# Attention and two expert layers on one core: scale and shift of the negated row maximum on ScalarE

## Chip, core, metric

The program runs on one core of a Trainium2 chip. The time is device microseconds of one execution; lower is better. TensorE (PE) multiplies, VectorE (DVE), ScalarE (ACT) and GpSimd (POOL) work element by element, SyncE (SP) issues the transfers (DMA).

## What is computed

Attention over 4 batches, 8 heads, 576 positions and 64 columns per head, with a mask by blocks of 64 positions, then a mixture of 4 expert layers on the 2304 x 512 result, then a second layer with a softmax, a normalisation and a last product. Of the attention, cut to what matters:

```python
scores = scale * np.matmul(q, k.transpose(0, 1, 3, 2))       # scale = 1/8
scores = np.where(mask, scores, -1000000000.0)
scores = scores - np.max(scores, axis=-1, keepdims=True)
attn = np.exp(scores)
attn = attn / (np.sum(attn, axis=-1, keepdims=True) + 1e-09)
return np.matmul(attn, v)
```

## The kernel before

The 2304 rows are 18 tiles of 128. Attention walks through 84 steps, `Attention.steps`. A step is a tile and some of its heads: four heads for the two tiles of first blocks (4 steps), two heads for tiles with index 1 to 3 (48 steps), one head for tiles with index 4 (32 steps).

A step goes through three functions. `step_a` has PE write the scores into a PSUM tile `sps` (`ps`; its pool `pss` has two buffers) and then, in its inner function `rest`, has DVE take the negated row maximum into the small tile `nm` (lines 923, 925, 927) and, on line 928, multiply it by 1/8 and add 14 ln 2, in place. `step_b` has ACT write exp(scores/8 + nm) into `p32` (line 959; the pool `pp` has two buffers), with the row sum as a second, small instruction; then ACT copies it as the high half into the f16 tile `hl` (line 963), DVE writes the low half by a subtraction (line 964, which frees the `p32` buffer), and SP issues a transposing transfer of `hl` into `pT`. `step_c` has PE multiply `pT` by the values (line 993, tile `pv`), one or two steps later, and `finish` normalises a tile and hands it to the expert layers.

A loop after the class weaves these steps with the units of the first expert phases (lines 372, 382, 383 for the hidden layer, lines 394, 414, 419 for its output), and with loading and splitting the weights (lines 129, 140, 232, 235 and, on POOL, 228). This woven part lasts until about 505 us. After it come the other expert phases and the second layer, which hold no attention.

Each engine runs its own queue in order. The order of a queue is not the order of the source: the context is opened with `schedule_with_timeline_sim=True`, so a planner lays out the queues by priority and by its own simulated times, and sets the semaphores. The evacuations of the expert layers have a raised priority (`tc.high_priority(offset=PRI)`). PE's `psh` pool for the hidden layer has three PSUM buffers.

Of the kernel before, what the change touches and what calls it, by code (L numbers as in the profile page):

```python
# [7 lines left out]
F32 = mybir.dt.float32  # L8
# [6 lines left out]
AF = mybir.ActivationFunctionType  # L15
ALU = mybir.AluOpType
# [7 lines left out]
SCALE = 1.0 / HD ** 0.5  # L24
BIG = 2.0 ** 50
PRI = 2000
PBITS = 14
LSC = 2.0 ** 10
OLAG = 4
LN2 = 0.6931471805599453  # L30
# [30 lines left out]
def tile_kernel(  # L61
# [38 lines left out]
    vec, act, gp, sync = nc.vector, nc.scalar, nc.gpsimd, InOrder(nc.sync)  # L100
    NPH = 3

    cp = ctx.enter_context(tc.tile_pool(name="const", bufs=1))
# [16 lines left out]
    pt = cp.tile([128, NTILE, E], F32, name="pt")  # L120
    iw = cp.tile([128, 18], F32, name="iw")
    gl = cp.tile([128, KF], F32, name="gl")
    x2i = cp.tile([128, NTILE], F32, name="x2i")

    def squares(x, out, junk=None):
# [615 lines left out]
    class Attention:  # L741
# [136 lines left out]
        def step_a(self, n):  # L878
            t, p, heads, _ = self.steps[n]
            b, i = TILES[t]  # L880
            ps = self.pss.tile([128, 2, 512], F32, tag="s", name="sps")
            self.sPS[n] = ps
            nm = sp.tile([128, 4], F32, tag="nm", name="nm")
            self.nm_[n] = nm
            nh = len(heads)
            L = 64 + 128 * i
            mms = []
            if i == 0:
                v4 = ps[:, 0].rearrange("p (h c) -> p h c", h=4)
                hi, lo = self.qS[t, p]  # L890
                ks = self.kS["z", b, p]
                for h in range(4):
                    o = v4[:, h]
                    pe.matmul(o, hi[:, h], ks[:, h], start=True, stop=False)
                    pe.matmul(o, lo[:, h], ks[:, h], start=False, stop=False)
                    pe.matmul(o, mr, mc, start=False, stop=True)
            else:
                for j, h in enumerate(heads):
                    even = h % 2 == 0
                    hi, lo = self.qS[t, h // 4]  # L900
                    k0 = S - L if even else 0
                    if i < 4:
                        cuts = [(ps[:, j, 0:L], k0, L)]
                    else:
                        cuts = [(ps[:, a, 0:288], k0 + 288 * a, 288) for a in range(2)]
                    for x, (o, c, w) in enumerate(cuts):
                        rhs = self.kS[b, h][:, c:c + w]
                        masked = (x == 0) if even else (x == len(cuts) - 1)
                        om = o[:, 0:64] if even else o[:, w - 64:w]

                        def high(o=o, q=hi[:, h % 4], rhs=rhs):
                            pe.matmul(o, q, rhs, start=True, stop=False)  # L912

                        def low(o=o, q=lo[:, h % 4], rhs=rhs, masked=masked, om=om):
                            pe.matmul(o, q, rhs, start=False, stop=not masked)  # L915
                            if masked:
                                pe.matmul(om, mr, mc[:, 64:128], start=False, stop=True)

                        mms += [high, low]

            def rest():
                if i == 0:
                    vec.tensor_reduce(out=nm, in_=v4, axis=AX.X, op=ALU.max, negate=True)
                elif i < 4:
                    vec.tensor_reduce(out=nm[:, 0:2], in_=ps[:, :, 0:L], axis=AX.X, op=ALU.max, negate=True)
                else:
                    vec.tensor_reduce(out=nm[:, 0:1], in_=ps[:, :, 0:288], axis=AX.XY, op=ALU.max, negate=True)
                vec.tensor_scalar(  # L928
                    out=nm[:, 0:nh], in0=nm[:, 0:nh], scalar1=SCALE, scalar2=PBITS * LN2, op0=ALU.mult, op1=ALU.add
                )  # L930

            return mms, rest

# [256 lines left out]


    vec.memset(ones, 1.0)

    vec.memset(mr, 0.0)
    vec.memset(mc, 0.0)
# [385 lines left out]
```

## Time and profile before

| | us |
|---|---|
| median of 3 runs (1112.07 to 1114.56) | 1113.18 |
| the profiled execution | 1114.37 |
| its span, first to last instruction | 1112.6 |
| PE busy | 1048.0 (94%) |
| DVE busy | 797.7 (72%) |
| ACT busy | 514.1 (46%) |
| POOL busy | 182.1 (16%) |

The profiled execution took 1.77 us more than its span and lies 1.19 us above the median. Timeline rows give the start, the duration, the engine, line and operation, the tiles (written <- read), shapes and count, and in brackets how long the engine stood idle before it and what ended that. `PEclk` is the granted TensorE clock as a share of full speed. The chain is the work that ended last, followed back from the last instruction.

### The profile page before, as it was taken

To read this page: it belongs to the slowest core of one execution; us is meant where nothing else is said; L and a number is where in the kernel's file an instruction comes from. 1 tells how busy PE (TensorE), PEld (TensorE's weight loads), DVE (VectorE), ACT (ScalarE), POOL (GpSimd) and SP (SyncE) were. 2 spreads that over 40 slices of the span, in tenths; PEclk is the share of its full clock that TensorE was granted. 3 is DMA by queue.
4 is the path that set the end of the run, shared out by engine and by line. 5 is a ranking of instruction groups with operands and counts; after the bars stand their busy time and mean duration, and the time that the engine had idled before them with its cause. 6 is when DMAs were issued, how large, how long until landed. Compare 5 with 4: busy or idle time off the path is not lost.

```text
span 1112.6 us, 20532 instructions
## 1 busy us (share of the span) xinstructions
PE 1048.0 (94%) x8064; PEld 657.2 (59%) x8064; DVE 797.7 (72%) x1758; ACT 514.1 (46%) x1107; POOL 182.1 (16%) x176
## 2 busy tenths in 40 slices
PE   4579889799999999999999999999999999999998
PEld 4456666465555556555576767666667674444443
DVE  7898788738768677436677656674879558999883
ACT  5667676646755455433443424232446453333222
POOL 4874633422115421000000000000000000000000
PEclk9999989799999999999999999999999999999999
DMA  9868987928877857332531212330344311434333
GB/s 303 247 164 159 249 184 163 222 79 192 193 120 178 177 147 157 64 61 48 174 114 58 77 39 76 115 133 29 95 138 128 107 27 29 95 86 88 74 85 85
DMA packets 225600, 137.95 MB, mean 124 GB/s; under 512 B 184544, under 2 KB 192736, under 8 KB 225504
## 3 DMA queue, kind: packets, MB, share of 16 engines
q1 hardware_dynamic: 225504, 136.65, 50.2%
q8 instruction: 63, 1.03, 0.4%
q14 instruction: 33, 0.27, 0.1%
HBM read 79.47 MB, written 12.06 MB: 82 GB/s over the span
## 4 chain that ended last, share of the span: by engine, by line
PE 75%; DMA 9%; DVE 7%; POOL 4%; issue 2%; ACT 2%; SPq 0%; ACTq 0%; DVEq 0%; POOLq 0%
PE ops L394 29%; PE hps L626 13%; PE hps L372 11%; PE h L1432 8%; PE o L1495 8%; DMA pT<-hl 6%; PE pv L993 3%; PE sps L912 2%; DVE hl L964 1%; PE sps L915 1%; DVE wt L235 1%; POOL wt L228 1%; DMA spill<-acc 1%; POOL ks L792 1%; POOL qlo L792 1%
## 5 line engine op out<-in xcount | busy, mean ns | idle before, releaser
L394 PE MATMUL ops<-wt,hch 128*128 128x512 f16 x1728 | 396.1, 381 | 3.7 <-DVE wt L235 1.6
L394 PEld LDWEIGHTS <-hch 128*128 128x128 f16 x1728 | 166.8, 98 | 189.9 <-issue 11.0
L372 PE MATMUL hps<-xT,wt 128*128 128x384 f16 (+1 forms) x1536 | 216.3, 291 | 2.1 <-DVE hch L383 1.3
L372 PEld LDWEIGHTS <-wt 128*128 128x128 f16 x1536 | 126.9, 100 | 62.1 <-issue 6.7
L959 ACT ACTIVATE p<-sps,nm 128x320 f32<-128x320 f32 (+4 forms) x144 | 79.0, 553 | 78.3 <-DVE nm L928 58.7
L964 DVE TENSOR_TENSOR hl<-p,hl 128x320 f16<-128x320 f32 (+4 forms) x132 | 92.3, 718 | 30.4 <-ACT hl L963 29.8
L626 PEld LDWEIGHTS <-S 128*128 128x128 f16 x1152 | 96.0, 98 | 2.8 <-issue 0.5
L1432 PE MATMUL h<-wt,x2T 128*128 128x512 f16 x432 | 95.5, 379 | 1.8 <-DVE acc L419 1.8
L1495 PE MATMUL o<-wt,lt 128*128 128x512 f16 x432 | 95.5, 379 | 0.0
L235 DVE SCALAR_TENSOR_TENSOR wt<-stage,ws,wt 128x1024 f16<-128x1024 f32 (+1 forms) x64 | 85.3, 1346 | 6.1 <-ACT wt L232 4.4
L419 DVE SCALAR_TENSOR_TENSOR acc<-ops,coef,acc 128x512 f32<-128x512 f32 x54 | 40.4, 747 | 67.2 <-PE ops L394 67.1
L912 PE MATMUL sps<-ks,qhi 128*128 128x288 f32 (+3 forms) x160 | 70.6, 443 | 18.1 <-ACT p L959 7.8
L639 ACT ACTIVATE stu<-hps 128x384 f32<-128x384 f32 x72 | 34.5, 484 | 94.7 <-PE hps L626 94.6
L626 PEld LDWEIGHTS <-wt 128*128 128x128 f16 x864 | 72.9, 98 | 6.5 <-issue 0.6
L626 PE MATMUL hps<-T,S 128*128 128x192 f16 x864 | 76.5, 246 | 0.0
L383 DVE SCALAR_TENSOR_TENSOR hch<-hps,hch 128x384 f16<-128x384 f32 (+1 forms) x98 | 53.0, 541 | 29.8 <-ACT hch L382 29.6
L1432 PEld LDWEIGHTS <-x2T 128*128 128x128 f16 x432 | 42.3, 98 | 52.9 <-issue 2.1
L993 PE MATMUL pv<-v,pT 128*128 128x64 f16 x1392 | 54.8, 196 | 19.1 <-DMA pT<-hl 19.0
L1495 PEld LDWEIGHTS <-lt 128*128 128x128 f16 x432 | 42.3, 98 | 51.0
L382 ACT ACTIVATE hch<-hps 128x384 f16<-128x384 f32 (+1 forms) x98 | 47.1, 480 | 47.7 <-PE hps L372 47.4
L232 ACT ACTIVATE wt<-stage,ws 128x1024 f16<-128x1024 f32 (+1 forms) x56 | 59.8, 1094 | 18.8 <-DVE ws L140 15.2
L993 PEld LDWEIGHTS <-pT 128*128 128x128 f16 x1392 | 50.1, 100 | 30.1 <-DMA pT<-hl 23.0
(158 smaller groups left out, 1480.6 us busy)
## 6 DMA issues: line engine op xcount, KB each, us to landing
stage<-in_w_dram SPq DMA_DIRECT2D x50, 512.0 KB, 6.0
raw<-in_qT_dram SPq DMA_DIRECT2D x34, 256.0 KB, 3.4
vraw<-in_vC_dram SPq DMA_DIRECT2D x30, 256.0 KB, 3.3
raw<-in_kT_dram SPq DMA_DIRECT2D x24, 288.0 KB, 3.6
raw<-in_w_dram SPq DMA_DIRECT2D x24, 256.0 KB, 4.0
raw<-in_w_in_dram SPq DMA_DIRECT2D x8, 512.0 KB, 4.7
raw<-in_w_out_dram SPq DMA_DIRECT2D x8, 512.0 KB, 4.3
stage<-wf SPq DMA_DIRECT2D x8, 512.0 KB, 6.1
```

The lines of the kernel that those rows point to most:

```text
L232: h = paced_a(bg_(act.activation(out=hi, in_=r, func=AF.Copy, scale=stage[key, "s"]), "A"))
L235: stage["last"] = vec.scalar_tensor_tensor(out=lo, in0=r, scalar=stage[key, "s"], in1=hi, op0=ALU.mult, op1=ALU.subtract)
L372: pe.matmul(ps[:, j * n:j * n + n], w[:, a, kk, f * 128:(f + 1) * 128], x[:, b * KD + kk, c0:c0 + n], start=(m == 0), stop=(m == 3 * KD - 1),)
L383: marks["D"] = nc.vector.scalar_tensor_tensor(out=h[:, 1, :n], in0=ps[:, :n], scalar=0.0, in1=h[:, 0, :n], op0=ALU.max, op1=ALU.subtract)
L394: pe.matmul(ps, hch[f][:, a, o0:o0 + 128], w[:, b, f, :], start=(m == 0), stop=(m == 3 * KF - 1))
L626: i = pe.matmul(ps[x][:, jj * HT:jj * HT + HT], lhs(a, kk, jj), rhs(b, kk), start=start, stop=(m == 5), skip_group_check=not first or jj > 0,)
L912: pe.matmul(o, q, rhs, start=True, stop=False)
L959: act.activation(out=dst, in_=src, func=AF.Exp, bias=nm[:, j + x:j + x + 1], scale=SCALE, accum_out=sums[:, h:h + 1],)
L964: anc["D"] = vec.tensor_tensor(out=hl[:, W + c0:W + c0 + n_], in0=pf[:, 0:n_], in1=hl[:, c0:c0 + n_], op=ALU.subtract)
L993: pe.matmul(o, tt[:, a * nch + c, :], v[:, bb, hs], start=(m == 0), stop=(m == total - 1))
L1432: pe.matmul(ps[:, half], x[:, a * KD + kk, c:c + 128], w[:, b, kk, half * 512:half * 512 + 512], start=(m == 0), stop=(m == 3 * KD - 1),)
L1495: pe.matmul(ps, tt[:, a * KF + f], w[:, b, f], start=(m == 0), stop=(m == 3 * KF - 1))
```

## The change

Line 928's VectorE instruction is taken out. In its place ScalarE runs an `Identity` activation on the same tile in place, with the same scale and with the shift read from a constant one-column tile `cb`, which VectorE fills once at the start. The maxima stay on VectorE, and the exponentials read `nm` as before.

```diff
+    cb = cp.tile([128, 1], F32, name="cb")
...
-                vec.tensor_scalar(
-                    out=nm[:, 0:nh], in0=nm[:, 0:nh], scalar1=SCALE, scalar2=PBITS * LN2, op0=ALU.mult, op1=ALU.add
-                )
+                act.activation(out=nm[:, 0:nh], in_=nm[:, 0:nh], func=AF.Identity, bias=cb, scale=SCALE)
...
     vec.memset(ones, 1.0)
+    vec.memset(cb, PBITS * LN2)
```

## Rows read from the trace of the kernel before

**Rows 1.** The page: PE's total, and the granted clock in 40 slices.

```profile
PE 1048.0 (94%) x8064; PEld 657.2 (59%) x8064; DVE 797.7 (72%) x1758; ACT 514.1 (46%) x1107; POOL 182.1 (16%) x176
PEclk9999989799999999999999999999999999999999
```

**Rows 2.** Busy time by stretch: engine and instructions, clock, DMA share, GB/s.

```profile
0.00:50.00 50.00, 21.59 (x132) 19.64 (x132) 39.05 (x92) 29.74 (x89) 31.86 (x39) 1.00 0.90 274
50.00:207.00 157.00, 132.73 (x1565) 99.72 (x1564) 128.48 (x253) 107.44 (x270) 85.84 (x76) 0.95 0.84 191
207.00:505.00 298.00, 292.53 (x2271) 169.67 (x2271) 191.34 (x396) 156.05 (x363) 64.44 (x63) 0.99 0.65 139
505.00:1112.60 607.60, 601.18 (x4102) 368.15 (x4100) 438.80 (x1019) 220.85 (x388) 0.00 (x0) 1.00 0.32 87
```

**Rows 3.** Line 928: durations (min/median/max, ns), and who waited for it (us, times).

```profile
L928 DVE TENSOR_SCALAR nm<-nm x84: 133/156/1220, 10.4 to 504.4; 128x2 f32<-128x2 f32 x48, 128x1 f32<-128x1 f32 x32, 128x4 f32<-128x4 f32 x4
  ACT p L959: 58.7, 31
```

**Rows 4.** ACT's groups by shape: busy us, mean ns, idle before.

```profile
L959 ACT ACTIVATE p<-sps,nm 128x576 f32<-128x576 f32 x32 | 23.6, 738 | 32.8 <-DVE nm L928 30.4 <-DVE x2i L137 1.0 <-DVE hl L964 0.9
...
L959 ACT ACTIVATE p<-sps,nm 128x128 f32<-128x128 f32 x16 | 5.7, 365 | 4.8 <-DVE nm L928 3.4 <-DVE vinv L133 0.8 <-PE sps L917 0.5
...
L788 ACT ACT_TABLE_LOAD x1 | 1.3, 1283 | 0.7 <-PEq L1570 0.7
```

**Rows 5.** Timeline of DVE at 367 us, then ACT: a step without a queue.

```profile
367.41 0.75 DVE L927 TENSOR_REDUCE nm<-sps 128x1 f32<-128x576 f32 x1
368.19 0.15 DVE L928 TENSOR_SCALAR nm<-nm 128x1 f32<-128x1 f32 x1
...
368.44 0.74 ACT L959 ACTIVATE p<-sps,nm 128x576 f32<-128x576 f32 x1 [1.83 <-DVE nm L928]
```

**Rows 6.** Timeline of DVE at 69 us, then ACT: a scale queued behind others.

```profile
69.47 0.81 DVE L925 TENSOR_REDUCE nm<-sps 128x2 f32<-128x640 f32 x1
...
74.58 0.97 DVE L928 TENSOR_SCALAR nm<-nm 128x2 f32<-128x2 f32 x1
...
75.64 0.53 ACT L959 ACTIVATE p<-sps,nm 128x320 f32<-128x320 f32 x1 [1.43 <-DVE xi L133]
```

**Rows 7.** Timeline of DVE at 85 us, then ACT: a scale behind a subtraction.

```profile
84.90 1.07 DVE L925 TENSOR_REDUCE nm<-sps 128x2 f32<-128x896 f32 x1
88.21 0.62 DVE L964 TENSOR_TENSOR hl<-p,hl 128x448 f16<-128x448 f32 x1 [2.23 <-ACT hl L963]
88.75 0.16 DVE L928 TENSOR_SCALAR nm<-nm 128x2 f32<-128x2 f32 x1
...
89.03 0.64 ACT L959 ACTIVATE p<-sps,nm 128x448 f32<-128x448 f32 x1 [0.39 <-DVE nm L928]
```

**Rows 8.** Timeline of DVE at 178 us, then ACT: ACT itself is queued.

```profile
178.56 0.16 DVE L928 TENSOR_SCALAR nm<-nm 128x2 f32<-128x2 f32 x1
...
179.73 0.71 ACT L1046 ACTIVATE xh<-xf,xs 128x512 f16<-128x512 f32 x1
180.34 0.62 ACT L959 ACTIVATE p<-sps,nm 128x448 f32<-128x448 f32 x1
```

**Rows 9.** The chain (start, us, what): first two and last piece of line 928.

```profile
14.56 0.58 DVE nm L928
...
74.66 0.57 DVE nm L928
...
185.51 0.08 DVE nm L928
```

**Rows 10.** Timeline of DVE at the start: the first work after the constants.

```profile
5.41 0.69 DVE L792 TENSOR_TENSOR kz<-kv,kz 64x512 fp32r<-64x512 f32 x1 [3.68 <-POOL kz L790]
```

**Rows 11.** PE's longest pause after 50 us, and the stretch around it as windows.

```profile
203.15 1.46 PE L993 MATMUL pv<-v,pT 128*128 128x64 f16 x24 [4.32 <-DMA pT<-hl]
...
197.90:211.60 13.70, 9.38 (x53) 6.33 (x53) 11.79 (x29) 11.63 (x24) 10.53 (x10) 0.50 1.02 217
```

## The prediction, made before the changed kernel was built or run

> **What bounds the kernel now.** I read the page first. PE is busy for 94% of the span, so a change off PE can only win where PE stands idle or slow [rows 1]. The digits of the granted clock tell that full speed was granted nearly throughout, with two dips, in slices 6 and 8, that is between 139 and 223 us [rows 1]. Next I cut the span into four stretches [rows 2]. From 505 us on there is no attention, and PE is busy for 601.18 of 607.6 us. From 207 to 505 us attention runs beside the expert layers, and PE is busy for 292.53 of 298 us. PE's idle time lies ahead of that: 28.4 of the first 50 us, and 24.3 of the 157 us from 50 to 207. In that second stretch DVE is busy for 128.48 of 157 us, ACT for 107.44, and the transfers take 0.84 of the DMA engines [rows 2]. So the edit can count between 0 and 207 us; behind that, PE's own work sets the pace.
>
> Then I asked for line 928 itself. It runs 84 times, its median is 156 ns and its longest 1220 ns, and in 31 places ACT's exponential stood idle for it, 58.7 us in all [rows 3]. That sum looks like the prize, and it is not: it counts the whole time for which ACT was idle, with the waiting for PE's scores and for the maximum in it, and most of it lies where ACT is not the bound.
>
> **The change part by part.**
>
> *Removed:* 84 small DVE instructions. In a step with free queues the maximum ends at 368.16 (367.41 + 0.75), the scale runs from 368.19 to 368.34, and the exponential starts at 368.44: 0.28 us from the end of the maximum [rows 5].
>
> *Added:* 84 ACT instructions of one to four columns. The trace has no such shape. The exponential, which also takes a scale and a column of biases, takes 738 ns for 576 columns and 365 for 128 [rows 4]; the straight line through these has 0.83 ns per column and meets zero columns at 258 ns. I take 0.26 us, an estimate from these two rows; it is bounded by 0.37 us above (the shortest exponential, [rows 4]) and 0.13 us below (the shortest scale on DVE, [rows 3]). With the 0.10 us of the hand-over that the rows show (368.34 to 368.44, [rows 5]) and 0.04 us more until the exponential can read the result, a free step would need 0.40 us in place of 0.28: each such step gets 0.12 us slower, not faster.
>
> The Trainium skill speaks against this change: "ScalarE: Activation LUTs", section Rules for kernel authors, wants multiplications and additions on VectorE. Its fixed price for an ACTIVATE with a column of biases, about 0.28 us, would make a free step 0.42 us, beside the 0.40 from rows; the trace agrees that a free step loses, and the sum below changes by 0.04 us.
>
> *What moves:* the gain can only come from steps where the scale was queued on DVE. In 53 of the 84 steps other DVE instructions stand between the maximum and its scale. At 69.47 the maximum starts and is done at 70.28, but the scale runs at 74.58 and takes 0.97 us; the exponential follows at 75.64 [rows 6]. Without the queue on DVE it could start about 1.3 us earlier, behind ACT's own work, which ends at about 74.2. At 84.90 it looks alike: the maximum is done at 85.97, the scale runs at 88.75. But ahead of it stands a subtraction of line 964 that had waited for ACT, and that subtraction ends at 88.83 and frees the `p32` buffer that the exponential at 89.03 writes [rows 7]. There the gain is 0.1 us, since the buffer comes when the scale came. And at 178.56 the scale was done at 178.72, while ACT was with other work until 180.44 and took the exponential at 180.34, overlapping it: there the new instruction only lengthens ACT's queue, by 0.27 us (0.26 and the hand-on) [rows 8].
>
> I went through all steps in this way: the new start is the latest of the end of the maximum plus 0.40, the buffer's release plus 0.10, and ACT's previous end plus 0.17 to 0.27. Of the 40 steps whose exponential starts before 207 us, 13 gain 9.9 us in all (0.1 to 2.9 each; [rows 6] is one), 22 lose 4.7 us in all (0.06 to 0.29 each; [rows 8] is one), and 5 don't move. After 207 us, 8 gain 4.5 and 34 lose 5.7 us, which PE's work hides.
>
> *On the chain:* the scale itself is there in six pieces, all before 207 us, 1.55 us together; the first two have 0.58 and 0.57, the last 0.08 [rows 9]. In the first two and the last one the chain goes on over DVE's queue and not over the exponential, so they go in full. Identity enters the chain where ACT's own queue is in it, at 180.34 with 0.27 us [rows 8], and in a place of the same kind at 93.9 with 0.20 us. In the other places it runs while the chain is with a subtraction of line 964, as in [rows 7], and that subtraction covers it; without that cover each would cost 0.26.
>
> *The constant:* one small fill on DVE more at the start. DVE then stands idle for 3.68 us until 5.41 [rows 10], so it costs nothing; without that cover it would cost about the 0.13 us of the shortest scale.
>
> *Sum:* 1.55 - 0.20 - 0.27 = 1.08 us less, so the span goes from 1112.6 to 1111.5 and that execution from 1114.37 to 1113.3. The median of the runs lies 1.19 us lower than the profiled execution, and I predict the median: 1113.18 - 1.08 = 1112.1 us. This kernel's measurement can tell about 0.2%, 2.2 us, from no change, so this is a forecast of "no difference", on the faster side.
>
> **The rivals.**
>
> *Faster: the early exponentials get through.* If the 9.9 us of earlier starts, less the 4.7 us of later ones, reach PE whole, 5.2 us are won: 1113.2 - 5.2 = 1108.0. For it: DVE is busy for 82% of 50 to 207 us, and the scale at 74.58 shows that it can cost DVE 0.97 us itself. Against it: an earlier exponential then waits for its buffers, as in [rows 7], and an earlier step for the same transfers into `pT`, on which PE's longest pause ends [rows 11]. There is a lever above that: PE's pause of 4.32 us at 198.8 is followed by half the clock (0.50, that is 1.2 GHz, from 197.9 to 211.6), which takes up to 6.8 us of PE's pace [rows 11]; if a shift of some tenths breaks that pause up, 1106 can be reached.
>
> *Slower: ACT's queue becomes the late link.* ACT takes its queue in order. Identity needs only the maximum, so the planner can put it ahead of work that used to run before the exponential; then ACT stands until DVE has reached that maximum, with evacuations of the hidden layer (line 382), copies of line 963 and weight squares queued behind, and PE waits for the first and the transfers for the second. ACT's work from 50 to 207 us also goes from 107.4 to 116 us (33 steps of 0.26). The price: the 4.7 us of later exponentials, with none of the gains, so 1113.2 + 4.7 = 1117.9. It decides from the point where more than a quarter of these delays (1.1 us, what the sum wins) reach a transposing transfer that is in the chain. For it: 22 of 40 steps have ACT queued. Against it: ACT is idle for 50 of these 157 us [rows 2].
>
> Which of these wins also hangs on the planner. Since 53 of 84 scales are not right behind their maximum, the queues do not follow the source, and taking out 84 and adding 84 instructions lays all of them out anew. A pause like that of [rows 11] lost or gained is 4 us either way; I let this widen the two rivals rather than shift the forecast.
>
> *Much slower: Identity is not among the loaded functions.* The trace loads a table once, 1283 ns, for copies, squares, exponentials and rectifications alike [rows 4]. If Identity needed another table, there would be two loads for each step: 40 x 2 x 1.28 = 103 us before 207 us, more than the slack of ACT there, and a time near 1200. The Trainium skill ("ScalarE: Activation LUTs", section Table sets: the hidden batching unit) names identity among the cheap functions that every set holds; no row shows Identity, but the one load for all the others fits that, so 0.02.
>
> **How the numbers follow.** Chances: forecast 0.40 (1110 to 1114.5), faster rival 0.30 (1105 to 1110), slower rival 0.28 (1115 to 1120), tables 0.02. Of the forecast's 0.40, 0.09 lies below 1111.0 and 0.02 above 1115.4. So faster by over 0.2%: 0.30 + 0.09 = 0.39; within: 0.29; slower: 0.28 + 0.02 + 0.02 = 0.32. For 8 in 10 the range takes the faster rival down to 1105.5 and the slower one up to 1118.5; the bounds of Identity (0.13 to 0.37 us in two places of the chain, 0.3 us either way) lie within it. The forecast's own range is 1110 to 1114.5.
>
> **What would show each step.** In the profile after, line 928's group should stand on ACT with 84 instructions of about 0.26 us, and one table load. A free step should show 0.40 us from the end of the maximum to the exponential. DVE's total should fall by at least 13 us (84 x 0.156), ACT's rise by up to 22 (84 x 0.26). If the forecast is right, PE's idle time from 50 to 207 us is still about 24 us, with pauses that end on `pT`; if the faster rival is, it is below 20 or the clock's dip at 198 us is gone; if the slower one is, ACT stands idle ahead of line 928 for a maximum with line 382 or 963 right behind, and PE's pauses grow. The prediction is wrong if PE's idle time after 207 us changes by more than 2 us, since I took that stretch as fixed.

## The result and the profile after

The changed kernel is slower: 1120.09 us median (4 runs, 1119.53 to 1122.79) beside 1113.71 for the kernel before (4 runs, 1112.07 to 1114.56), a ratio of 1.0064 with an interval of 1.0043 to 1.0084. The forecast was 1112.1 with a range of 1105.5 to 1118.5. The profiled execution took 1119.53 us, its span is 1117.7. Each experiment below was run beside new runs of the kernel before, whose median lay between 1114.64 and 1115.52 us; its ratio is to those.

The page after, the same two lines as in [rows 1], then the four stretches of [rows 2] in the same columns:

```profile
PE 1051.1 (94%) x8064; PEld 657.6 (59%) x8064; DVE 784.5 (70%) x1675; ACT 533.1 (48%) x1191; POOL 178.6 (16%) x176
PEclk9989999899999999999999999999999999999999
```

```profile
0.00:50.00 50.00, 22.51 (x134) 19.85 (x134) 39.31 (x86) 32.19 (x100) 33.48 (x41) 1.00 0.95 282
50.00:207.00 157.00, 131.66 (x1526) 97.03 (x1526) 118.54 (x216) 107.81 (x287) 76.72 (x70) 0.95 0.80 178
207.00:505.00 298.00, 291.40 (x2255) 169.73 (x2256) 186.62 (x354) 170.91 (x416) 68.44 (x67) 0.98 0.65 144
505.00:1117.70 612.70, 605.51 (x4151) 371.00 (x4149) 440.07 (x1021) 222.16 (x390) 0.00 (x0) 1.00 0.31 86
```

DVE has lost 13.2 us and ACT has gained 19.0, as the change says. The span grew by 5.1 us, and all of that is in the last row: 612.7 against 607.6 us from 505 us on, where nothing was touched. The counts tell why. Up to 207 us PE did 37 recorded matmuls fewer than before (134 + 1526 against 132 + 1565), from there to 505 us 16 fewer, and behind 505 us 49 more. The loss arises early and is paid at the end.

Next the new instruction itself: duration in ns (least, median, most), and what ended the idle time of ACT ahead of it (us, times); then ACT's groups by shape; then a step with free queues, as in [rows 5]:

```profile
L929 ACT ACTIVATE nm<-nm,cb x84: 278/295/298, 10.5 to 508.3; 128x2 f32<-128x2 f32 x48, 128x1 f32<-128x1 f32 x32, 128x4 f32<-128x4 f32 x4
...
  DVE nm L928: 30.1, 18
  DVE nm L926: 27.7, 20
```

```profile
L929 ACT ACTIVATE nm<-nm,cb 128x2 f32<-128x2 f32 x48 | 14.0, 291 | 27.7 <-DVE nm L926 27.7
...
L929 ACT ACTIVATE nm<-nm,cb 128x1 f32<-128x1 f32 x32 | 9.1, 291 | 30.1 <-DVE nm L928 30.1
...
L789 ACT ACT_TABLE_LOAD x1 | 1.3, 1283 | 0.7 <-PEq L1570 0.7
L929 ACT ACTIVATE nm<-nm,cb 128x4 f32<-128x4 f32 x4 | 1.2, 293 | 2.7 <-DVE nm L924 2.7
```

```profile
369.60 0.74 DVE L928 TENSOR_REDUCE nm<-sps 128x1 f32<-128x576 f32 x1
...
370.38 0.30 ACT L929 ACTIVATE nm<-nm,cb 128x1 f32<-128x1 f32 x1 [1.91 <-DVE nm L928]
370.71 0.74 ACT L958 ACTIVATE p<-sps,nm 128x576 f32<-128x576 f32 x1
```

A free step needs 0.37 us from the end of the maximum (370.34) to the exponential; it was 0.28. There is one table load, as before. So far everything is as forecast, and none of it is worth 6 us.

The orders of the queues are not as before. In the built programs 1631 of PE's 8048 instructions, 335 of DVE's 1674, 218 of ACT's 846, 35 of POOL's 172 and 70 of SP's 388 stand at another place, all within the attention part. If only the fill of `cb` is added to the kernel before, the built program has one instruction more and nothing moves. "Old order" below is the planner's order of the kernel before, "new order" that of the changed kernel.

What the new order does shows best at the 10th step, in the timeline after (the maximum on DVE, then ACT), and then in ACT's timeline of the first experiment, which runs the new instruction in the old order (there all operations stand at one line, so the tiles tell them apart):

```profile
69.59 0.82 DVE L926 TENSOR_REDUCE nm<-sps 128x2 f32<-128x640 f32 x1 [0.72 <-PE sps L918]
...
72.33 0.64 ACT L130 ACTIVATE vraw<-vraw 128x512 f32<-128x512 f32 x1 [8.46 <-DMA vraw<-in_vC_dram]
...
72.96 0.28 ACT L929 ACTIVATE nm<-nm,cb 128x2 f32<-128x2 f32 x1
74.29 0.63 ACT L130 ACTIVATE vraw<-vraw 128x512 f32<-128x512 f32 x1 [1.05 <-DMA vraw<-in_vC_dram]
...
74.92 0.51 ACT L958 ACTIVATE p<-sps,nm 128x320 f32<-128x320 f32 x1
```

```profile
65.10 0.30 ACT L156 ACTIVATE nm<-nm,cb 128x2 f32<-128x2 f32 x1 [1.08 <-DVE nm L156]
66.10 0.53 ACT L156 ACTIVATE p<-sps,nm 128x320 f32<-128x320 f32 x1 [0.70 <-DVE hl L156]
...
68.97 0.63 ACT L156 ACTIVATE vraw<-vraw 128x512 f32<-128x512 f32 x1 [1.39 <-DMA vraw<-in_vC_dram]
...
72.28 0.63 ACT L156 ACTIVATE vraw<-vraw 128x512 f32<-128x512 f32 x1 [2.23 <-DMA vraw<-in_vC_dram]
```

The `vraw` instructions square a tile of values and can start only when it has been transferred. In the old order the step's Identity and exponentials stand ahead of two such squares, which wait for transfers. In the new order the squares stand ahead of Identity and of the exponentials. ACT then stood idle for 8.46 us and, after Identity, 1.05 us more. The maximum was ready at 70.41 (69.59 + 0.82) and the exponential started at 74.92.

The chain of waits after (start, us, what) tells what made the transfer late. PE's pauses after stand below it, and last PE's longest pause of that stretch in the kernel before:

```profile
54.89 2.42 POOL wt L229 x2
57.31 2.09 POOL ks L791 x2
59.41 1.19 POOL wt L229
60.60 1.45 POOL ks L791
62.05 0.07 issue
62.12 3.45 POOL ks L793 x2
65.57 0.09 issue
65.67 1.55 POOL wt L229
...
67.30 2.11 POOL ks L793
69.41 0.02 issue
69.43 2.79 DMA vraw<-in_vC_dram
...
72.33 0.10 ACT vraw L130
...
73.07 2.85 DMA vraw<-in_vC_dram
...
79.49 5.12 DMA pT<-hl
84.61 0.05 issue
84.65 0.70 PE pv L992 x18
```

```profile
64.17 4.63 PE L395 MATMUL ops<-wt,hch 128*128 128x512 f16 x11 [4.70 <-POOL ks L793]
76.12 0.39 PE L913 MATMUL sps<-ks,qhi 128*128 128x320 f32 x1 [1.79 <-issue]
84.65 0.70 PE L992 MATMUL pv<-v,pT 128*128 128x64 f16 x18 [2.93 <-DMA pT<-hl]
```

```profile
62.09 1.67 PE L394 MATMUL ops<-wt,hch 128*128 128x512 f16 x7 [1.27 <-DVE hch L383]
```

POOL does splits of weights (`wt`) among its preparations of keys (`ks`), the value load goes out at 69.43 behind the last of these, ACT waits for it with the exponentials behind, and the transposing transfer and PE's `pv` follow. PE's pause of 4.70 us ends at 64.17, ahead of ACT's stall; those that end at 76.12 and 84.65 come behind it. The kernel before had its longest pause between 58 and 95 us at 62.09, with 1.27 us.

To see where PE falls back, a second number is used below: the time that PE has lost up to a point, that is the clock time less what the matmuls started by then take at a common pace (for each shape the fastest fifth of the start-to-start distances in the kernel before).

| lost by (us) | 50 | 87.5 | 150 | 1000 |
|---|---|---|---|---|
| before | 35.6 | 45.7 | 54.1 | 80.0 |
| after | 35.3 | 50.8 | 61.5 | 85.2 |

Beyond the kernel before, 5.1 us are gone by 87.5, 7.4 by 150, and 5.2 remain at 1000 us. The same count at points between gives 2.8 us by 65, behind the first pause, and 1.5 by 72.5, so ACT's stall is not the only source.

### The profile page after: what moved, and what is told of

It is laid out like the page before. It is cut to its first block, busy times and chain, and to the rows that moved or that the text cites. A ratio compares the mean times of both kernels' runs of the same rounds, so it can differ in the third digit from the quotient of the medians.

```text
span 1117.7 us, 20517 instructions
## 1 busy us (share of the span) xinstructions
PE 1051.1 (94%) x8064; PEld 657.6 (59%) x8064; DVE 784.5 (70%) x1675; ACT 533.1 (48%) x1191; POOL 178.6 (16%) x176
## 4 chain that ended last, share of the span: by engine, by line
PE 74%; DMA 9%; DVE 7%; ACT 3%; POOL 3%; issue 2%; SPq 0%; ACTq 0%; DVEq 0%; POOLq 0%
PE ops L395 29%; PE hps L627 13%; PE hps L373 10%; PE h L1432 8%; PE o L1495 8%; DMA pT<-hl 5%; PE pv L992 2%; DVE hl L963 1%; PE sps L913 1%; PE sps L916 1%; DMA vraw<-in_vC_dram 1%; DMA stage<-in_w_dram 1%; DVE v L875 1%; POOL wt L229 1%; POOL ks L793 1%
## 5 line engine op out<-in xcount | busy, mean ns | idle before, releaser
L963 DVE TENSOR_TENSOR hl<-p,hl 128x320 f16<-128x320 f32 (+4 forms) x132 | 89.2, 693 | 37.9 <-ACT hl L962 37.6
L236 DVE SCALAR_TENSOR_TENSOR wt<-stage,ws,wt 128x1024 f16<-128x1024 f32 (+1 forms) x64 | 85.2, 1340 | 6.9 <-ACT wt L233 4.8
L420 DVE SCALAR_TENSOR_TENSOR acc<-ops,coef,acc 128x512 f32<-128x512 f32 x54 | 40.4, 748 | 64.4 <-PE ops L395 64.3
L992 PE MATMUL pv<-v,pT 128*128 128x64 f16 x1392 | 55.6, 197 | 13.2 <-DMA pT<-hl 11.2
L962 ACT ACTIVATE hl<-p 128x320 f16<-128x320 f32 (+4 forms) x132 | 65.3, 522 | 5.8 <-DMA pT<-hl 5.2
L916 PE MATMUL sps<-ks,qlo 128*128 128x288 f32 (+3 forms) x160 | 62.9, 395 | 3.0 <-POOL qlo L793 3.0
```

The costliest lines, as they stand in the source:

```text
L236: stage["last"] = vec.scalar_tensor_tensor(out=lo, in0=r, scalar=stage[key, "s"], in1=hi, op0=ALU.mult, op1=ALU.subtract)
L962: anc["A"] = act.activation(out=hl[:, c0:c0 + n_], in_=pf[:, 0:n_], func=AF.Copy)
L963: anc["D"] = vec.tensor_tensor(out=hl[:, W + c0:W + c0 + n_], in0=pf[:, 0:n_], in1=hl[:, c0:c0 + n_], op=ALU.subtract)
L992: pe.matmul(o, tt[:, a * nch + c, :], v[:, bb, hs], start=(m == 0), stop=(m == total - 1))
```

## The experiments

Theory A: the instruction on ACT costs the time (the slower rival). Theory O: the orders that the planner laid out around it cost the time. To part them, the order of every engine's queue is held: each engine is wrapped so that its instructions are recorded, and each is made to follow the one ahead of it in a list that was read out of a built program.

```diff
-    pe = nc.tensor
+    pe = Rec(nc.tensor, "PE")
...
+                ins = f(*args, **kwargs)
+                log.append((self.key, ins))
...
+    for key, steps in zip(("PE", "DVE", "ACT", "POOL", "SP"), _j.loads(_z.decompress(_b.b85decode(ORDERS)))):
...
+            if last is not None:
+                after(log[at][1], last)
+            last = log[at][1]
```

**Instruction and order, parted.** Three runs with the lists

```diff
 e1: Identity on ACT, old order, Identity right ahead of its step's first exponential
 e2: scale on DVE right behind its maximum, new order
 e3: Identity on ACT, new order, but Identity right ahead of the first exponential
```

> The changed kernel (scale and shift as an Identity on ScalarE), with the order of every queue held as the planner laid it out for the kernel before: each engine's instructions are chained one behind the other, the 84 scales are taken out of VectorE's queue, and each Identity stands on ScalarE right ahead of its step's first exponential. Theory O (the 6 us come from the new order that the planner laid out, not from the instruction's new place): the time is that of the kernel before, 1113.7 us within 2. Theory A (the 6 us come from the instruction: 0.295 us more on ScalarE ahead of the exponentials, 0.08 us more in a free step): 1120 us within 2 in the old order too. In between: both share.

> The kernel before (scale and shift on VectorE), with the order of every queue held as the planner laid it out for the changed kernel; each scale stands on VectorE right behind its maximum, and the Identities are left out of ScalarE's queue. Theory O (the order costs the 6 us): about 1120 us, at least 1117. Theory A (the instruction on ScalarE costs them): 1113.7 us within 2, since the instruction is back on VectorE; with every scale right behind its maximum perhaps 1 us less.

> The changed kernel in its own order, but with each Identity moved on ScalarE's queue to stand right ahead of its step's first exponential (in 45 of 84 steps other ScalarE work stands between the two). Theory H (a part of the 6 us comes from Identities that stand far ahead and hold ScalarE's queue until VectorE has the maximum): 1116 us or less. Theory O, with the order of the other instructions to blame: unchanged, 1120 us within 1.5. Theory A: unchanged too or somewhat slower, since the Identity then always lies directly on the way to the exponential.

Measured: e1 1114.66 us, 0.9993 [0.9981, 1.0005]; e2 1123.73, 1.0076 [1.0054, 1.0097]; e3 1119.12, 1.0044 [1.0027, 1.0061]. The new instruction in the old order is as fast as the kernel before; the old instruction in the new order is as slow as the changed kernel, or slower. Theory A falls as the cause of the 6 us. The place of Identity within ACT's queue (e3) gives back about 2 us of the loss, and the interval overlaps that of the changed kernel. The cleanest pair is e1 and e3: the Identity stands right ahead of the first exponential in both, and the order of the rest alone costs 4.5 us by the medians and 5.7 by the ratios. One limit: in e2 the scale stands right behind its maximum and not where the planner would have put it.

In e2 there is no Identity, and the stall of the 10th step is there all the same:

```profile
73.03 0.63 ACT L157 ACTIVATE vraw<-vraw 128x512 f32<-128x512 f32 x1 [8.54 <-DMA vraw<-in_vC_dram]
...
74.89 0.63 ACT L157 ACTIVATE vraw<-vraw 128x512 f32<-128x512 f32 x1 [1.14 <-DMA vraw<-in_vC_dram]
...
75.52 0.51 ACT L157 ACTIVATE p<-sps,nm 128x320 f32<-128x320 f32 x1
```

**Twice the instruction.** In the old order, two ACT instructions in series for each step:

```diff
-                act.activation(out=nm[:, 0:nh], in_=nm[:, 0:nh], func=AF.Identity, bias=cb, scale=SCALE)
+                act.activation(out=nm[:, 0:nh], in_=nm[:, 0:nh], func=AF.Copy, scale=SCALE)
+                act.activation(out=nm[:, 0:nh], in_=nm[:, 0:nh], func=AF.Identity, bias=cb)
```

> The old order again, but with two ScalarE instructions in series for scale and shift (a Copy with the scale, then an Identity with the shift), both right ahead of the first exponential, so 0.3 us more on ScalarE in each of 84 steps than with one. Theory O (order): the instruction lies on the way in a few places only, 1115.5 us within 1.5. The slower rival of the forecast (ScalarE's queue is the late link, each late exponential reaches PE): 40 steps of up to 0.3 us ahead of 207 us, 1120 us or more.

Measured: 1115.97 us, 1.0015 [0.9996, 1.0035]. By the ratios that is 2.5 us more than e1, for 84 more instructions of 195 ns on the way to the exponentials, with intervals that overlap. The slower rival expected 1120 us or more here. Its delays of 4.7 us reach PE in part at most.

**Where in the new order.** The same new instruction, the order changed over at the maximum of the 10th or the 25th step:

```diff
 h1: new order up to the 10th maximum, then old
 h2: new order up to the 25th maximum, then old
 h3: old order up to the 25th maximum, then new
 h4: old order up to the 10th maximum, then new
 h5: new order between the 10th and the 25th maximum alone
```

> The changed kernel, its queues in the planner's new order up to the maximum of the 10th attention step (about 70 us), and in the old order from there on. Theory F (the cost arises in the first 70 us, where PE pauses 4.70 us at 59.5 in the changed kernel, at half the clock behind it): 1119 us or more, against 1114.7 with the old order throughout. Theory M (it arises in steps 10 to 24, up to about 135 us, where PE's lost time grows from 2 to 8 us beyond that of before): 1116 to 1117. Theory L (later): 1115 or less. Theory N (no one place: each joint of two orders has a time of its own): no sum comes out of the hybrids.

> As the one before, with the new order up to the maximum of the 25th step (about 135 us) and the old order behind it. Theory F: 1119 or more, no higher than with the cut at step 10. Theory M: 1119 to 1122, some 3 us above the cut at step 10. Theory L: 1115 or less. The trace of the changed kernel (8 us of lost PE time at 150 us, 4.7 at 500) would make it 1120.

> The complement: old order up to the maximum of the 25th step, new order behind it. Theories F and M: 1114.7 or less, since what costs lies ahead of the cut; by the trace of the changed kernel, which wins back 3 us behind 150 us, perhaps 1112. Theory L: 1119 or more. Theory N: any time, with the two halves not adding up to the 5 us between the old and the new order.

> The changed kernel with the old order up to the maximum of the 10th attention step and the new order from there on. Theory S (the new order costs between the 10th and the 25th step and nowhere else): as the changed kernel or up to 2 us less, 1118 to 1121. Theory J (the 1126.8 of the new order up to the 25th step came from the joint, and the new order costs by its first 70 us, which all later steps carry on): 1112 to 1115.

> Old order, new order only between the maxima of the 10th and the 25th step, old order again. Theory S: 1120 us or more. Theory J: 1116 us or less, unless the second joint costs by itself, as with the new order up to the 25th step; then the trace shows the loss of PE's time behind 135 us and not ahead of it.

Measured, with PE's lost time, the start of the 10th maximum and of its first exponential. The last four columns come from one profiled execution each, which for e2 and h2 was the fastest of its runs (1118.70 and 1122.27 us):

| | us | ratio | lost by 87.5 | by 150 | by 1000 | 10th maximum, exponential |
|---|---|---|---|---|---|---|
| e1, old order | 1114.66 | 0.9993 [0.9981, 1.0005] | 45.9 | 56.0 | 80.8 | 64.3, 66.1 |
| h1 | 1116.62 | 1.0021 [1.0003, 1.0039] | 47.9 | 56.1 | 82.3 | 69.6, 70.8 |
| h3 | 1112.28 | 0.9977 [0.9959, 0.9995] | 45.7 | 54.3 | 77.8 | 63.5, 65.4 |
| after | 1120.09 | 1.0064 [1.0043, 1.0084] | 50.8 | 61.5 | 85.2 | 69.6, 74.9 |
| e2 | 1123.73 | 1.0076 [1.0054, 1.0097] | 49.8 | 60.8 | 84.3 | 69.6, 75.5 |
| h2 | 1126.78 | 1.0106 [1.0080, 1.0131] | 48.3 | 63.0 | 87.1 | 69.0, 74.2 |
| h4 | 1120.73 | 1.0044 [1.0026, 1.0061] | 50.2 | 61.5 | 83.9 | 70.8, 75.8 |
| h5 | 1124.41 | 1.0086 [1.0062, 1.0110] | 49.4 | 64.4 | 91.2 | 71.0, 76.0 |

The cost sits between the 10th and the 25th step: of these eight, every kernel with the new order there is 0.44% or more slower, and of the others none is by more than 0.21%. The five slow ones have 5.0 to 5.9 us from the start of the 10th maximum to its exponential, the others 1.2 to 1.9. In h4 the old order ahead of the stretch leaves the stall in place, and it is longer:

```profile
73.99 0.63 ACT L157 ACTIVATE vraw<-vraw 128x512 f32<-128x512 f32 x1 [10.97 <-DMA vraw<-in_vC_dram]
...
74.62 0.28 ACT L157 ACTIVATE nm<-nm,cb 128x2 f32<-128x2 f32 x1
```

The parts don't add up: behind the joint at which they change back to the old order h2 and h5 lose more than the kernel after (10.4 and 9.8 us of lost time between 137.5 and 162.5 us, against 7.0), so their size is partly that of the joint. Behind the 25th step the new order is perhaps better than the old one: h3 is the fastest kernel of this case, but its interval and that of e1 overlap.

**Expert work ahead of scores (theory K).** On PE the new order has expert matmuls ahead of scores that stood behind them in the old one, up to 14.7 us of them at the 17th step. If that is the cost, scores that the planner must put first should give it back.

```diff
+                            with tc.high_priority(offset=200):
-                            pe.matmul(o, q, rhs, start=True, stop=False)
+                                pe.matmul(o, q, rhs, start=True, stop=False)
```

(e7: the changed kernel with offset 50; e8: with 200; e9: the kernel before with 200.) The planner lays these out itself. With them ran e10, the kernel before's instructions in a third order, the one that the planner lays out if scale and shift are two DVE instructions.

> The changed kernel, laid out by the planner itself, with one edit: the score matmuls of attention have their priority raised by 50. In the changed kernel the planner set up to 14.7 us more of expert matmuls ahead of a step's scores on PE's queue than in the kernel before (57.0 against 42.3 us at the 17th step, 81.6 against 70.5 at the 22nd), and the 42nd maximum, behind which PE never waits long, came 6.8 us later (214.2 against 207.4). With the raised priority the 17th step has 43.7 us ahead and the 22nd 74.5. Theory K (expert work taken ahead of the scores makes attention late, and is missing when PE has nothing else at the 37th to 42nd step): the 42nd maximum at 208 to 210 us and 1112 to 1116 us. Theory N (any new layout is a draw, the expert work ahead of the scores says nothing): anywhere from 1110 to 1124, with no tie to the 42nd maximum.

> As e7, with the priority of the scores raised by 200: less expert work still stands ahead of the scores than in the kernel before (4.7 us against 15.6 at the 10th step, 62.2 against 64.5 at the 21st, 132.2 against 140.0 at the 39th). Theory K: no later than the kernel before, 1108 to 1114 us, unless the expert work left over then lacks evacuation behind 240 us. Theory N: no tie.

> The kernel before (scale and shift on VectorE) with the priority of the scores raised by 200; up to 2 us of expert work less ahead of the scores than in e8 at some steps, more at others. Theory K: 1108 to 1114 us, within 2 us of e8, since the instruction's place does not matter and the layouts are alike. Theory A (the instruction on ScalarE costs time): 4 to 6 us under e8.

> The kernel before, its queues held in a third order: the one that the planner lays out when VectorE does scale and shift in two instructions (2198 of PE's 8048 matmuls then stand elsewhere). The instructions are those of the kernel before. Theory N and theory K alike: another time than 1114.7, by up to 10 us either way; theory K: later than before if its 42nd maximum comes later than 207 to 210 us, by as much. If the order did not matter: 1114.7 within 2.

Measured: e7 1119.28 us, 1.0035 [1.0017, 1.0053]; e8 1123.99, 1.0077 [1.0055, 1.0100]; e9 1124.62, 1.0086 [1.0061, 1.0111]; e10 1126.37, 1.0098 [1.0071, 1.0125]. In e8 the 25th maximum started at 131.6 us, as early as before (130.8), and the kernel is no faster for it. So scores first are no remedy; the 1108 to 1114 us that theory K expected of e8 and e9 did not come. Whether expert work ahead of the scores is part of the cause stays open: by the same count as above e8 has lost 3.1 us more than the kernel before by 150 us, where the kernel after has 7.4, and its loss grows from 1.0 at 200 to 8.7 at 1000 us, so it pays elsewhere. The place of the instruction shows no difference between e8 and e9, where theory A expected 4 to 6 us; there the planner chose it for both, in layouts that are alike but not equal. What the four show beside that: each further layout of nearly the same work is slower than that of the kernel before, by 0.35 to 0.98%. None of these four shows the stall of 8 us at the 10th step (e10 has one of 4.5 us), so it isn't the only way to lose.

**GpSimd's queue alone (theory G).** In the chain after, the weight splits on POOL stand first. Sixteen of POOL's instructions there, or all of them, were exchanged between the two orders.

```diff
 e11: new order, 16 GpSimd instructions in their old order
 e12: old order, the same 16 in their new order
 e13: new order, all of GpSimd in the old order
 e14: old order, all of GpSimd in the new order
```

> The changed kernel in its new order, but with 16 of GpSimd's 172 instructions (numbers 40 to 55, about 54 to 75 us) in the order of before: the keys of the next steps then stand ahead of three of four weight splits. Theory G (this stretch of GpSimd's queue makes the first late steps, and with them the 5 us): the 10th maximum at 64 to 66 us and not at 69.6, and 1114 to 1116.5 us. Theory D (the cost is spread over the queues; the first stretch is made up for later): 1119 or more, though the 10th maximum comes earlier.

> The changed instruction in the old order, with the same 16 instructions of GpSimd in the new order, weight splits first. Theory G: the 10th maximum 3 to 5 us later than with the old order (64.3 us), and 1117 to 1120 us. Theory D: within 2 of the old order's 1114.7.

> As e11, with the whole of GpSimd's queue in the old order; 35 of its 172 instructions stand elsewhere than in the new order, 19 of them outside the stretch of e11. Theory G: as e11 or up to 1 us better. Theory D: 1119 or more.

> As e12, with the whole of GpSimd's queue in the new order. Theory G: as e12 or up to 1 us worse. Theory D: within 2 of 1114.7.

Measured: e11 1124.37 us, 1.0083 [1.0055, 1.0110]; e12 1116.32, 1.0012 [0.9996, 1.0029]; e13 1124.54, 1.0085 [1.0056, 1.0113]; e14 1120.35, 1.0064 [1.0039, 1.0089]. Theory G falls for the sixteen: the old queue of POOL doesn't cure the new order, and the sixteen alone don't harm the old one. But e14 fits neither expectation: all of POOL's new queue makes the old order as slow as the changed kernel. What the rest of that queue does wasn't taken apart. In e11 the weights now come late, PE waits for the hidden layer, and the 10th maximum starts only at 76.3 us:

```profile
66.47 4.39 PE L157 MATMUL ops<-wt,hch 128*128 128x512 f16 x11 [6.68 <-DVE hch L157]
```

Argued from e11, e13 and e14, and not shown: the queues of one layout fit each other, and to exchange one of them makes a new loss. PE's, DVE's or ACT's queue can't be exchanged alone, because the queues then wait for each other in a circle.

**The old instruction in the best order.** The kernel before's scale, right behind its maximum, in the order of h3:

```diff
 e15: scale on DVE, old order up to the 25th maximum, then new
```

> The kernel before (scale and shift on VectorE) in the order of the fastest kernel so far: old order up to the maximum of the 25th step, new order behind it. Theory O (the order decides, the instruction's place does not): 1112.3 us within 2, as with the instruction on ScalarE. Theory A (the instruction on ScalarE costs): 3 us or more below that.

Measured: 1119.65 us, 1.0046 [1.0025, 1.0067], where h3 has 0.9977. With e1 against before and after against e2, that is the third pair of one order in which the instruction on ACT is no slower than on DVE. But the 1112.3 us that theory O expected did not come: in this order the instruction on ACT is faster by 0.7%, so its place is not without effect in every order. The trace shows where the loss begins, with one execution of each: the scale at 54.68 takes 1.02 us on a DVE that is busy without a break from 49.4 us on, DVE comes to its part of the hidden layer at 64.15 (60.78 in h3), and PE waits for that, where in h3 it waited for 1.27 us:

```profile
64.75 3.05 PE L157 MATMUL ops<-wt,hch 128*128 128x512 f16 x7 [4.25 <-DVE hch L157]
```

The limit of e2 holds here too: the scale stands at a place that the planner didn't choose, and whether DVE's work or that place costs the time isn't shown.

## Why the prediction was wrong

**The step that failed** is the one on the planner: the new layout was written down as "4 us either way", to widen the two rivals and not to shift the forecast. So it stood in the sum at nothing, and it was nearly the whole result. The sum, made with the old layout, could not hold for the changed kernel. The size was not far off: with the instruction on ACT the order costs 4.5 us by the medians of e1 and e3 (5.7 by the ratios); with the scale on DVE (e2) it is some 8.5 us, of which the scale's place may be a part. "Either way" was wrong here: of the layouts that the planner made (after, e7, e8, e9 and e10), none came out faster than that of the kernel before.

**Bound and stretch** held. PE stays the bound, and its idle time behind 207 us is 13.8 us against 11.9 (6.60 + 7.19 from the windows after, 5.47 + 6.42 from [rows 2]); 1.9 us more is just within the 2 us that were set as the sign of an error. That the loss shows there as time of the last stretch doesn't contradict it: it is work left over. The sign that was set for the forecast came too, some 24 us of idle time of PE from 50 to 207 us (25.3 against 24.3), without the forecast's time: PE also lost pace at the lower clock (last section), which idle time doesn't show.

**The instruction's cost** was a little low: 291 to 295 ns for a forecast of 0.26 us, within the bounds of 0.13 and 0.37. The free step came out at 0.37 us, not 0.40, since the hand-overs are shorter than put down: 0.04 us from the maximum to Identity and 0.03 from Identity to the exponential. DVE's fall of 13.2 us met the 13 forecast, ACT's rise is 19.0 of at most 22. The Trainium skill ("ScalarE: Activation LUTs", section Rules for kernel authors) wants such work on VectorE. The trace agrees for a free step, which got slower by 0.09 us, and e1 shows that the kernel's time doesn't feel it. In the order of h3 and e15 VectorE was the slower place, with the limit said there.

**The sum on the chain** of -1.08 us is not contradicted: e1, which is the change without a new layout, is at -0.8 us, with an interval from -2.1 to +0.6. It can't be told from nothing, and so the terms (1.55, 0.20 and 0.27) are not each shown. The fill of the constant costs nothing and moves nothing; the single table load was right.

**The faster rival** (early exponentials reach PE, 5.2 us) didn't come; in e1 they had the old order, and at most 2.1 us came. **The slower rival** came near in number (1117.9), which is luck, and in the main not in mechanism. It had Identity wait for its maximum with evacuations queued behind. In the trace it is the other way about: Identity and the exponentials stand behind a square of values that waits for a transfer, and e2 has the same without Identity. What is left of its mechanism is at most the 2 us or so that e3 gives back. The extra time on ACT, which was to be its price, is bounded by e4.

**Two slips of the working.** The half clock of [rows 11] was said to follow the pause of 4.32 us; by the rows it is there from 197.9 us, and the pause begins at 198.83 (203.15 - 4.32). So to break up that pause need not have removed the dip. And the forecast's own range ends at 1114.5, though 0.02 of its chance was put above 1115.4.

**What stays open.** That the order costs the time is shown, and that what costs in the new order sits in steps 10 to 25. That the stall at the 10th step is its main part is not shown. It is read from the traces: after, e2, e3, h2, h4 and h5 have the exponential late behind the squares, and before, e1, e4, h1 and h3 don't. For it: h1 has PE's first pause (4.04 us until 63.93) without the stall and has lost 2.2 us more than the kernel before by 87.5; h4 has the stall without that pause and has lost 4.5. Against it: e7 has lost 5.3 us more by 87.5 without the stall, e8, e9, e14 and e15 are slow without it, and in e11 and e13 ACT stands as long for such a square (9.68 and 9.82 us), but ahead of a maximum that is itself late. No run changed that one place alone. What adds 2 to 3 us more up to 150 us was not taken apart.

## What to carry to other kernels

Where a planner lays out the queues, moving one small instruction to another engine is two changes: the instruction, whose price can be estimated from rows, and a new order of everything around it, whose price nobody could read from the rows here. Compare the orders of the two programs first, or hold the old one, and take the measured spread between layouts of equal work (here -0.2 to +1.1%) as the width of the forecast; it lay mostly on the slow side. In a queue that runs in order, look for what stands ahead of the moved instruction, above all work that waits for a transfer.

## What the runs showed of the hardware

An Identity with a column of biases takes the same for one, two and four columns (291, 291 and 293 ns); a Copy with a constant scale on the same tiles took 195 ns in e4 (median of 84). So between one and four columns the price is fixed, and the form counts more than the columns.

TensorE's clock fell to half (0.50, that is 1.2 GHz) beside PE's pauses in the kernel after too. PE stood idle until 64.17 and until 84.65 (rows above), and these stretches overlap or follow (us, PE, PEld, DVE, ACT and POOL busy, granted clock, DMA share, GB/s). Below them stand the sums of all stretches at half the clock, six after and then three before:

```profile
61.60:68.40 6.80, 4.24 (x11) 1.52 (x12) 6.33 (x13) 2.17 (x6) 6.53 (x5) 0.50 0.41 92
85.50:88.90 3.40, 3.40 (x18) 2.07 (x17) 1.98 (x5) 1.44 (x6) 0.00 (x0) 0.50 0.64 140
...
sum 27.20, PE 23.45 PEld 15.15 DVE 20.84 ACT 18.12 POOL 11.51; mean PE 3.91 PEld 2.53 DVE 3.47 ACT 3.02 POOL 1.92
```

```profile
sum 23.90, PE 18.76 PEld 13.82 DVE 18.13 ACT 19.08 POOL 12.31; mean PE 6.25 PEld 4.61 DVE 6.04 ACT 6.36 POOL 4.10
```

In all, 27.2 us of the kernel after ran at half the clock, and 23.9 us of the kernel before; PE was busy for 23.45 and 18.76 us of them. In this trace the 512-column matmuls of line 395 started 427 ns apart at half the clock and 216 ns apart at full clock (medians), so about half of that busy time is the price of the clock: 11.7 and 9.4 us, an estimate from these numbers. Some 2.3 us of the 5.1 us longer span would then be the clock's. A loss doesn't need it, though: e9 is slow (1.0086) at a mean granted clock of 0.990, where the kernel before in the same group had 0.989. The dip of [rows 11] at 198 us, which the faster rival hoped to break up, stands at 208.4 us in the kernel after, with half its length.
